# A long convolution and a spectral mixer on one core: two Z blocks share one buffer for their upper 52 rows, which are contracted in pairs of half height

## The chip, the cores and the metric

The kernel runs on one core of one Trainium2 chip. The metric is the device time of one execution in microseconds. A core has TensorE (PE; its weight loads are listed as PEld), VectorE (DVE), ScalarE (ACT), GpSimd (POOL), and SyncE (SP), which issues DMA transfers here. Sixteen DMA engines serve the core.

## The reference

The input x has 8 batches of 5696 positions and 128 channels. The first part is a causal convolution along the sequence with a filter h as long as the sequence, written as a product of spectra. The second part mixes the 64 lowest modes of the result's spectrum with complex 128 x 128 matrices, adds the mixed signal y to the convolution's result to get u, and returns u plus the positive part of u times a matrix.

```python
def _attn_ref(x, h):
    L = 2 * S
    Yf = np.fft.rfft(x, n=L, axis=1) * np.fft.rfft(h, n=L, axis=0)[None]
    return np.fft.irfft(Yf, n=L, axis=1)[:, :S]

def _moe_ref(x, w_r, w_i, w_ch):
    X = np.fft.rfft(x, axis=1)
    Xr, Xi = X.real[:, :64], X.imag[:, :64]
    Yr = einsum('bmd,mde->bme', Xr, w_r) - einsum('bmd,mde->bme', Xi, w_i)
    Yi = einsum('bmd,mde->bme', Xr, w_i) + einsum('bmd,mde->bme', Xi, w_r)
    u = x + np.fft.irfft(Yr + 1j * Yi, n=S, axis=1)
    return u + np.maximum(u @ w_ch, 0.0)
```

## The kernel before

The sequence index is split as 64 times 89. The batches go in four groups of two. For each group the kernel transforms along the 89 positions (As), then along the 64 (Xs), multiplies by the filter's spectrum (U), transforms back along the 64 (Z), and writes Z to a scratch tensor `zscr` in DRAM as 2 x 90 = 180 rows (real and imaginary parts of 90 frequencies) of 64 positions x 256 columns (two batches of 128 channels). A write covers four frequencies, so 23 of them, one per "tick", fill a group. On the way the 64 low modes of each batch are collected (XT). All four groups pass through these ticks; this ends at about 249 us.

**The last stage.** The modes are mixed with the weights (`mix`, result C), and then the convolution's result is made by contracting the 180 rows of Z with a constant table S4, while C times a table IBs adds the mixed modes into the same PSUM banks. The 64 positions of a group go in four *blocks* of ZB = 16 positions, so there are 16 blocks in all. A block's 180 rows do not fit the 128 partitions: rows 0 to 127 stand in a buffer ZT*a and rows 128 to 179 (RB = 52 rows) in ZT*b, from partition PB = 32 on. The 32 partitions below are cleared once by POOL (`clear_zt`), and the contraction of this part runs over 84 partitions. There are NC = 5 buffers of each kind. `load_zt(i)` issues the two transfers of a block on SP.

A *tile* (`u_tile`, called with the block, the batch b and the half) makes 8 positions in two PSUM banks: `u_c` gives one matmul with C for each bank, and `u_z` for each of the 8 positions one S4a matmul over 128 rows and one S4b matmul over 84 rows, each with 89 columns. ScalarE or VectorE then moves the tile to a buffer UT in SBUF, in runs of 8 elements. Sixteen tiles make a group. When a group's tiles are done, its output is made by `o_tile`: four matmuls with WI (the channel matrix beside an identity), the positive part on ScalarE (R), the sum on VectorE (O or Os), and a transfer to the output. These output tiles are interleaved with the tiles of the next group, one or two after each tile, by the list `todo`. There are seven large output buffers O, each holding two output tiles and written by one transfer of 512 KB, and four small ones Os.

Tiles rotate through four slots of two PSUM banks, which output tiles share. Engines work in order. Each reads its own list, and waits are semaphores that a recorder derives from what an operation reads and writes. SP too is in order: a load behind an output transfer that waits for VectorE waits as well. A load waits until its buffer's last reader on TensorE is done.

**What runs ahead.** The tables and the first blocks are loaded during the ticks of the last group, by the dictionary `early`: at tick 8 the table S4b, at tick 10 block 0, at tick 12 S4a, at tick 14 the identity Id and IBs, at tick 16 block 1, then blocks 3 and 2; block 4 follows after the ticks. The load of Id waits for two of the Z writes to land, so SP stands still there for a while. Only half of S4 and IBs is loaded; the other half follows by symmetry and is made on the chip by `reflect`, on VectorE for S4a and IBs and on ScalarE for S4b. Three tiles of block 0 are contracted ahead of C, in between the matmuls of `mix` (`u_z` with `alone`).

The order of a tile before is, for each bank, C and then S4a and S4b in turn:

```python
for hb in parts:
    if not alone:
        u_c(i, b, half, t, hb, True)
    for pl in range(4):
        for ri in range(2):          # S4a, S4b
            ...
            mm(pv(t + hb, pl * NQ, [[1, NQ]]), z[ri][0:n, ...], s4_sb[ri][0:n, so:so + NQ], ...)
```

Of the kernel before, what the change touches and what calls it, by code (L numbers as in the profile page):

```python
# [4 lines left out]
P = 128  # L5
F16 = mybir.dt.float16
# [117 lines left out]
def bass_long_conv_fft__then__afno_spectral_mix_kernel(nc, x, h, moe_w_r, moe_w_i, moe_w_ch, out):  # L124
# [37 lines left out]
    s4t = np.zeros((P, 2 * SH))  # L162
    s4t[:, 0:SH] = rows[0:P, 0:SH]
    s4t[PB:PB + RB, SH:2 * SH] = rows[P:2 * NK, 0:SH]
    sg = np.ones((P, 3))
    sr = np.stack([(-1.0) ** kk, -(-1.0) ** kk], axis=1).reshape(2 * NK)
    sg[:, 0] = sr[0:P]
    sg[PB:PB + RB, 1] = sr[P:2 * NK]
    sg[M:P, 2] = -1.0
    tt = np.arange(S)  # L170
# [38 lines left out]
    def take(nbytes):  # L209
# [40 lines left out]
    wc_sb = at("Wc", 2 * P, F16, take(2 * P * 2))  # L250
    sg_sb = at("SG", 3, F32, take(12))
# [4 lines left out]
    ZB = 16  # L256
# [4 lines left out]
    zt_off = [(a_h, a_h2), (a_as1, a_as1 + 2 * ZP), (a_as1 + 4 * ZP, a_as1 + 6 * ZP), (a_h + 2 * ZP, a_h2 + 2 * ZP),  # L261
              (a_m2, a_g)]
    assert 2 * S + 8 * ZP <= AW * 2
    zt = [[at(f"ZT{i}{'ab'[p_]}", ZP, F16, zt_off[i][p_]) for p_ in range(2)] for i in range(NC)]
    ib_sb = at("IBs", S, F16, a_m)
    s4_sb = [at("S4a", S, F16, a_m + 2 * S), at("S4b", S, F16, a_as)]
    assert 4 * S + 2 * ZP + 4 * P + 2048 <= 2 * MW
# [27 lines left out]
    R = Recorder(nc)  # L295
    for name, n in (("c", 16), ("x", 26), ("z", 10), ("w", 16), ("t", 20), ("s", 8), ("o", 12), ("p", 16), ("q", 10)):
        R.ring(name, n)
# [229 lines left out]
    ZX = [("zs", i, b) for i in range(NZ, NZL) for b in range(2)]  # L527
    zt_old = [(H_ALL, H_ALL), (AST, AST), (AST, AST), (H_ALL, H_ALL), (M_ALL[3:6], G_ALL)]

    def load_zt(i):  # L530
        g_, c_ = divmod(i, J // ZB)
        for part, (p0, r0, n) in enumerate(((0, 0, P), (PB, P, RB))):
            old = list(once(("zt", i % NC, part), zt_old[i % NC][part]))
            dma("sync", bass.AP(zt[i % NC][part], p0 * ZP, [[ZP, n], [1, ZP]]),
                bass.AP(zs, (g_ * 2 * NK + r0) * J * 256 + c_ * ZB * 256, [[J * 256, n], [1, ZP]]),
                "t", [("zd", g_, s_) for s_ in range(NT)], [("zt", i % NC, part)], after=old)

    def clear_zt(i):
        z32 = zt[i][1][0:PB, :].bitcast(U32)
        R.add("gpsimd", lambda e: e.memset(z32, 0), (), [("zt0", i)], after=list(zt_old[i][1]) + pace)  # L540

    def load_ib():
# [11 lines left out]
    def load_s4(part):  # L554
        n = PB + RB if part else P
        dma("sync", s4_sb[part][0:n, 0:SH], bass.AP(c_s4, part * SH, [[2 * SH, n], [1, SH]]), "p", (),
            [("s4", part, 0)], after=AST if part else M_ALL[1:4])
# [13 lines left out]
    pace = []  # L571

# [91 lines left out]
    def tick(g_, t):  # L664
# [27 lines left out]
        if LC <= t < NT + LC:  # L692
            s_ = t - LC
            n = len(ticks[s_])
            i, zi = s_ % NU, zroom(g_, s_)
            zb = [turns("z", ZBANK) for b in range(2)]
            for b in range(2):
                for r in range(2):
                    mm(pv(zb[b], 0, [[1, n * D]]), (W1, W2)[r], u_s[i][:, r * 1024 + b * 512:r * 1024 + b * 512 + n * D],
                       r == 0, r == 1, [("u", i), ("wc",)], [bank(zb[b])])  # L700
                evac(bass.AP(z_s[zi], b * D, [[1024, P], [2 * D, n], [1, D]]),
                     pv(zb[b], 0, [[D, n], [1, D]]), [bank(zb[b])], [("zs", zi, b)], eng="scalar",
                     after=once(("zx", zi, b), Z_OLD) if zi >= NZ else ())
                if b == 0:
                    drained(g_, t, 0)
            zo = (g_ * NK + KT * s_) * P * 256
            dma("sync", bass.AP(zs, zo, [[256, P], [P * 256, n], [1, 256]]),
                bass.AP(z_s[zi], 0, [[1024, P], [256, n], [1, 256]]), "z",
                [("zs", zi, 0), ("zs", zi, 1)], [("zd", g_, s_)])
# [39 lines left out]
    for g_ in range(NP):  # L749
# [3 lines left out]
        for t in range(NT + LM):  # L753
            tick(g_, t)
            assert g_ + 1 < NP or not wp
            if g_ == NP - 1 and t in early:
                pace[:] = [("u", min(t, NT - 1) % NU)]
                early[t]()
# [13 lines left out]

    pace[:] = []
    load_wi()
    for i in range(4, NC):
        load_zt(i)
        clear_zt(i)

# [4 lines left out]

    def u_z(i, b, half, alone=False, parts=(0, 1)):
        g_, c_ = divmod(i, NCH)
        t = ahead.get((i, b, half))
        if t is None:
            t = turns("l", LSLOT)
        z = zt[i % NC]
        for hb in parts:  # L790
            if not alone:
                u_c(i, b, half, t, hb, True)
            for pl in range(4):
                for ri in range(2):
                    pz = half * 8 + hb * 4 + pl
                    so = (c_ * ZB + pz) * NQ
                    n = (P, PB + RB)[ri]
                    mm(pv(t + hb, pl * NQ, [[1, NQ]]), z[ri][0:n, pz * 256 + b * P:pz * 256 + b * P + P], s4_sb[ri][0:n, so:so + NQ],
                       alone and pl == 0 and ri == 0, not alone and pl == 3 and ri == 1, [("zt", i % NC, ri), ("zt0", i % NC), ("s4", ri, 0)] + ([("s4", ri, 1)] if c_ >= NCH // 2 else []), [bank(t + hb)])
        if alone:  # L800
            ahead[(i, b, half)] = t
        return t

    def u_c(i, b, half, t, hb, first_):
        g_, c_ = divmod(i, NCH)
        pl0 = half * 8 + hb * 4
        mm(pv(t + hb, 0, [[1, 4 * NQ]]), c_sb[:, (2 * g_ + b) * P:(2 * g_ + b + 1) * P],
           ib_sb[:, (c_ * ZB + pl0) * NQ:(c_ * ZB + pl0 + 4) * NQ], first_, not first_,
           [("c", g_ // 2), ("ib", 0)] + ([("ib", 1)] if c_ >= NCH // 2 else []), [bank(t + hb)])

    def u_tile(i, b, half):
        g_, c_ = divmod(i, NCH)
        t = ahead.get((i, b, half))
        if t is None:
            t = u_z(i, b, half)
        else:
            for hb in range(2):
                u_c(i, b, half, t, hb, False)
        ub = (g_ % 2) * 2 + b
# [3 lines left out]
        src = pv(t, 0, [[1, NQ], [512, 2], [NQ, 4]])  # L823
        evac(bass.AP(u_sb[ub], c_ * ZB + half * 8, [[S, P], [J, NQ], [4, 2], [1, 4]]),
             src, [bank(t), bank(t + 1)], [("u_", ub, 2 * c_ + half)], eng=e, after=once(("u", ub), old))
# [32 lines left out]
    reflect("vector", ib_sb, P, 2, ("ib",), M_ALL[0:2])  # L858

# [52 lines left out]
    todo = []  # L912
    NB = NCH * NP
    NW4 = NW // 4
    for g_ in range(NP):
        last = g_ == NP - 1
        order = [(c_, b) for b in range(2) for c_ in range(NCH)] if last else [(c_, b) for c_ in range(NCH) for b in range(2)]
        for n, (c_, b) in enumerate(order):
            i = NCH * g_ + c_
            for half in range(2):  # L920
                u_tile(i, b, half)
                for _ in range((2, 2 + half)[n >= NCH] if last else 1 + half):
                    if todo:
                        o_tile(*todo.pop(0))
            if b == 1 and i + NC < NB:
                load_zt(i + NC)
            if last and n == NCH - 1:
                todo += [(g_, 0, r4) for r4 in range(NW4)]
# [37 lines left out]
```

## Time and profile before

| | us |
|---|---|
| Time, median of 3 runs | 372.31 (371.18 to 373.6) |
| Span of the profiled execution, first to last instruction | 370.1 |
| TensorE busy | 354.7 (96%) |
| ScalarE busy | 316.2 (85%) |
| VectorE busy | 291.8 (79%) |
| POOL busy | 75.2 (20%) |
| Chain that ended last: TensorE's share | 78% |

The profile is one execution; the runs were timed without it. A matmul's length in it reaches from its start to its modelled end, and matmuls overlap in the pipe, so the price of one is the distance between starts. The granted TensorE clock was 0.999 on average. Numbers behind "x" are counts.

### The profile page before, as it was taken

How to read it: one execution, taken by the hardware profiler on the slowest of the kernel's cores; microseconds unless marked ns; L12 is line 12 of the kernel's file. 1: busy time of each engine (PE TensorE's matmuls, PEld its weight loads, DVE VectorE, ACT ScalarE, POOL GpSimd, SP SyncE). 2: the span in 40 equal slices, each digit the busy share in tenths (PEclk: the TensorE clock that was granted, in tenths of full speed). 3: DMA queues.
4: the chain of work that ended last, by engine and by line, in shares of the span. 5: the costliest groups of instructions: out<-in, count | busy, mean ns of one | idle time of the engine just before them, and what ended most of it. 6: DMA issues, size and time to landing. Idle time of an engine off the chain costs nothing.

```text
span 370.1 us, 12455 instructions
## 1 busy us (share of the span) xinstructions
PE 354.7 (96%) x5350; PEld 276.5 (75%) x5350; DVE 291.8 (79%) x332; ACT 316.2 (85%) x499; POOL 75.2 (20%) x117
## 2 busy tenths in 40 slices
PE   7999899999999999999999999999999999999994
PEld 7878766667866668866668766668899888888873
DVE  3549899988999999989999988775357777756666
ACT  8559999999999999999999999995467777688885
POOL 8804012100833311823213001151000000000000
PEclk9999999999999999999999999999999999999999
DMA  7999979969999996999996999999999999999878
GB/s 139 209 271 382 249 165 292 232 198 283 93 140 213 263 258 186 132 160 215 263 278 128 171 310 363 342 345 388 381 410 386 413 410 408 418 399 376 326 291 349
DMA packets 87048, 103.94 MB, mean 281 GB/s; under 512 B 22730, under 2 KB 72522, under 8 KB 83438
## 3 DMA queue, kind: packets, MB, share of 16 engines
q1 hardware_dynamic: 64610, 81.33, 62.5%
q0 software_dynamic: 22384, 21.83, 35.4%
q8 instruction: 42, 0.69, 0.7%
q14 instruction: 12, 0.10, 0.1%
HBM read 70.61 MB, written 51.12 MB: 329 GB/s over the span
## 4 chain that ended last, share of the span: by engine, by line
PE 78%; ACT 10%; DMA 7%; DVE 3%; issue 1%; POOL 1%; DVEq 0%; POOLq 0%
PE ps L323 78%; ACT As L313 6%; DMA out_dram<-O 5%; DMA Hin<-in_h_dram 2%; ACT R L898 1%; DVE As L317 1%; ACT Xs L311 1%; DVE U L623 1%; POOL Hin L320 1%; ACT UT L311 1%; DVE O L899 0%; ACT Zs L311 0%; DVE Hp L438 0%; ACT C L313 0%; DVE Hs L315 0%
## 5 line engine op out<-in xcount | busy, mean ns | idle before, releaser
L652 DVE TENSOR_TENSOR U<-Xs,Hs 128x2048 f16<-128x2048 f16 (+1 forms) x72 | 85.8, 1197 | 12.1 <-ACT Xs L311 11.5
L323 PE MATMUL ps<-U,Wc 128*128 128x512 f16 (+1 forms) x368 | 93.8, 376 | 1.4 <-DVE U L623 1.4
L311 ACT CAST Xs<-ps 128x1024 f16<-128x1024 f32 (+1 forms) x76 | 75.0, 995 | 5.8 <-PE ps L323 3.1
L311 ACT CAST Zs<-ps 128x512 f16<-128x512 f32 (+1 forms) x132 | 70.1, 605 | 0.7
L899 DVE TENSOR_TENSOR O<-ps,R 128x512 f32<-128x512 f32 x81 | 52.4, 684 | 21.6 <-ACT R L898 11.4
L898 ACT ACTIVATE R<-ps 128x512 f32<-128x512 f32 (+1 forms) x92 | 50.5, 592 | 8.5 <-PE ps L323 8.4
L317 DVE TENSOR_SCALAR As<-ps 128x720 f16<-128x720 f32 x64 | 53.1, 879 | 4.8 <-PE ps L323 3.3
L323 PE MATMUL ps<-As,M 64*128 64x128 f16 (+3 forms) x1504 | 52.5, 214 | 2.4 <-ACT As L313 1.2
L313 ACT ACTIVATE As<-ps 128x720 f16<-128x720 f32 (+1 forms) x68 | 48.2, 771 | 5.0 <-PE ps L323 4.8
L323 PE MATMUL ps<-F,Xin 128*128 128x180 f16 x512 | 52.1, 249 | 0.1
L323 PE MATMUL ps<-WI,UT 128*128 128x256 f16 x360 | 50.8, 278 | 0.5 <-ACT UT L311 0.4
L311 ACT CAST UT<-ps 128x712 f16<-128x712 f32 x46 | 34.5, 752 | 19.4 <-PE ps L323 18.4
L323 PEld LDWEIGHTS ps<-U,Wc 128*128 128x128 f16 x368 | 29.1, 97 | 28.2 <-DVE U L623 1.9
L323 PEld LDWEIGHTS ps<-F,Xin 128*128 128x128 f16 x512 | 45.2, 155 | 6.7 <-DVE Xin L365 0.9
L323 PEld LDWEIGHTS ps<-As,M 64*128 64x128 f16 x1504 | 42.2, 94 | 8.7 <-ACT Xs L311 1.9
L323 PEld LDWEIGHTS ps<-WI,UT 128*128 128x128 f16 x360 | 38.9, 152 | 3.2 <-issue 1.8
L323 PE MATMUL ps<-IBs,C 128*128 128x356 f16 x128 | 39.2, 314 | 0.8 <-DVE O L899 0.7
L320 POOL DMA_DIRECT2D Xt<-in_x_dram x40 | 21.4, 540 | 76.5 <-PE ps L323 76.0
L323 PEld LDWEIGHTS ps<-G,Zs 128*128 128x128 f16 x512 | 26.1, 96 | 14.1 <-ACT Zs L311 0.2
L652 DVE TENSOR_TENSOR U<-ps,Hs 128x2048 f16<-128x2048 f32 (+1 forms) x16 | 35.5, 2216 | 0.0
L323 PE MATMUL ps<-G,Zs 128*128 128x128 f16 (+2 forms) x512 | 31.9, 192 | 0.1
L311 ACT CAST Zt<-ps 128x512 f16<-128x512 f32 x52 | 29.1, 659 | 0.0
(76 smaller groups left out, 479.4 us busy)
## 6 DMA issues: line engine op xcount, KB each, us to landing
out_dram<-O SPq DMA_DIRECT2D x39, 512.0 KB, 10.5
zscr<-Zs SPq DMA_DIRECT2D x62, 256.0 KB, 6.7
zscr<-Zt SPq DMA_DIRECT2D x26, 256.0 KB, 6.6
Xt<-in_x_dram POOLq DMA_DIRECT2D x20, 320.0 KB, 6.9
W<-wscr SPq DMA_DIRECT2D x4, 1024.0 KB, 8.5
ZT0a<-zscr SPq DMA_DIRECT2D x4, 1024.0 KB, 11.0
M<-cM POOLq DMA_DIRECT2D x5, 720.0 KB, 17.6
ZT1a<-zscr SPq DMA_DIRECT2D x3, 1024.0 KB, 11.1
```

Of the source, the lines that this page charges most:

```text
L311: R.add(e, lambda h_: h_.copy(dst, src), reads, writes, after=after)
L313: R.add(e, lambda h_: h_.activation(dst, src, COPY, scale=scale), reads, writes, after=after)
L317: R.add(e, lambda h_: h_.tensor_scalar_mul(dst, src, scale), reads, writes, after=after)
L320: R.add(eng, lambda h_: h_.dma_start(dst, src), reads, writes, ring=ring, after=after)
L323: R.add("tensor", lambda h_: h_.matmul(o, l, r, start=st, stop=sp), reads, writes)
L623: R.add("vector", lambda e: e.tensor_tensor(bass.AP(u_s[0], b * 512 + d0, [[2048, P], [1024, 2], [D, n], [1, d1 - d0]]), bass.AP(s_[0], s_ ...
L652: R.add("vector", lambda e: e.tensor_tensor(uv, src, hv, MULT), bk + [("h", t, 0), ("h", t, 1, 0), ("h", t, 1, J)], [("u", i)])
L898: R.add("scalar", lambda e: e.activation(rv, src_r, RELU), bk, [("r", i % NR)], after=once(("r", i % NR), G_ALL + XTT + [("y", 0), ("y", 1 ...
L899: R.add("vector", lambda e: e.tensor_tensor(ov, src_u, rv, ADD), bk + [("r", i % NR)], [key + (h_,)], after=once(key, old))
```

## The change

- The upper 52 rows of two neighbouring blocks share one buffer ZB*: block 2k from partition 0, block 2k+1 from partition PB = 64. There are NCB = 3 such pair buffers, and NCA = 7 buffers ZA* for the lower 128 rows of single blocks.
- A tile now covers 4 positions of each of the two blocks of a pair instead of 8 positions of one, so a pair has 8 tiles. Its order is: C for both banks, four S4a matmuls for the one block, four for the other, and then for each position the two S4b matmuls, one on partitions 0-51 and one on 64-115, one behind the other. Each of these has 52 rows and is built for a half-height (64-row) position of the array.
- The table S4b is laid out to match, over S/2 columns and both partition halves, and is loaded whole. Its reflection on ScalarE is gone, and so are the clears on POOL.
- The last write of each group (tick 22, two frequencies, 4 rows) goes to a scratch tensor of its own, `zlast`, whose pieces of 256 elements stand 264 apart. A pair buffer is therefore loaded, for each of its two blocks, by one transfer of 48 rows and four transfers of one row in sixteen pieces of 512 bytes: ten transfers for a pair. They use a ring "r" of 16 semaphores of their own.
- The loads move: at tick 10 ZA for block 0 and the first pair buffer, at tick 16 ZA for block 1, at tick 19 ZA for block 2 and the second pair buffer, at tick 21 ZA for block 3, after the ticks ZA for block 4, the third pair buffer, and ZA for blocks 5 and 6. Later, at the end of each pair, the next pair buffer and two ZA.
- UT is written in runs of 4 elements, 16 apart, instead of runs of 8.

```diff
-    RB, PB = 2 * NK - P, 32
+    RB, PB = 2 * NK - P, 64
+    RS = RB % 16
...
+    for p0 in range(2):
+        s4b[p0 * PB:p0 * PB + RB] = rows[P:].reshape(RB, J // ZB // 2, 2, ZB * NQ)[:, :, p0].reshape(RB, S // 2)
...
+    ZLW = 2 * D + 8
+    zl = nc.dram_tensor("zlast", [NP * RS * J, ZLW], F16, kind="Internal")
...
-    NC = 5
+    NCA, NCB = 7, 3
...
-    def load_zt(i):
...
-    def clear_zt(i):
...
+    def load_za(i):
+        g_, c_ = divmod(i, J // ZB)
+        r_ = i % NCA
+        dma("sync", za[r_][:, :], bass.AP(zs, g_ * 2 * NK * J * 256 + c_ * ZP, [[J * 256, P], [1, ZP]]),
+            "t", zdone(g_), [("za", r_)], after=once(("za", r_), za_old[r_]))
+
+    def load_zb(k):
+        r_ = k % NCB
+        for p0 in range(2):
+            g_, c_ = divmod(2 * k + p0, J // ZB)
+            n = RB - RS
+            dma("sync", bass.AP(zb_[r_], p0 * PB * ZP, [[ZP, n], [1, ZP]]),
+                bass.AP(zs, (g_ * 2 * NK + P) * J * 256 + c_ * ZP, [[J * 256, n], [1, ZP]]),
+                "t", zdone(g_), [("zb", r_, p0)], after=once(("zb", r_, p0), zb_old[r_]))
+            for r in range(n, RB):
+                dma("sync", bass.AP(zb_[r_], (p0 * PB + r) * ZP, [[ZP, 1], [256, ZB], [1, 256]]),
+                    bass.AP(zl, ((g_ * RS + r - n) * J + c_ * ZB) * ZLW, [[J * ZLW, 1], [ZLW, ZB], [1, 256]]),
+                    "r", zdone(g_), [("zr", r_, p0, r)], after=once(("zr", r_, p0, r), zb_old[r_]))
...
-             9: lambda: clear_zt(0),
-             10: lambda: load_zt(0),
+             10: lambda: (load_za(0), load_zb(0)),
              12: lambda: load_s4(0),
-             14: lambda: (load_id(), load_ib(), clear_zt(1)),
-             16: lambda: load_zt(1),
-             19: lambda: (load_zt(3), clear_zt(3)),
-             NT - 2: lambda: (load_zt(2), clear_zt(2))}
+             14: lambda: (load_id(), load_ib()),
+             16: lambda: load_za(1),
+             19: lambda: (load_za(2), load_zb(1)),
+             NT - 2: lambda: load_za(3)}
...
+        for hb in range(2 if 0 in parts else 0):
+            z, r_ = za[(2 * k + hb) % NCA], (2 * k + hb) % NCA
             for pl in range(4):
...
+                mm(pv(t + hb, pl * NQ, [[1, NQ]]), z[:, pz * 256 + b * P:pz * 256 + b * P + P], s4_sb[0][:, so:so + NQ],
+                   alone and pl == 0, False, [("za", r_)] + ns, [bank(t + hb)])
+        r_ = k % NCB
+        for pl in range(4 if 1 in parts else 0):
...
+            for hb in range(2):
+                r0 = hb * PB
+                mm(pv(t + hb, pl * NQ, [[1, NQ]]), zb_[r_][r0:r0 + RB, pz * 256 + b * P:pz * 256 + b * P + P],
+                   s4_sb[1][r0:r0 + RB, so:so + NQ], False, not alone and pl == 3,
+                   [("zb", r_, hb), ("s4", 1, 0)] + [("zr", r_, hb, r) for r in range(RB - RS, RB)], [bank(t + hb)])
...
-    reflect("scalar", s4_sb[1], PB + RB, 1, ("s4", 1), AST)
...
             if b == 1:
+                if k + NCB < NPR * NP:
+                    load_zb(k + NCB)
+                for i in (2 * k, 2 * k + 1):
+                    if i + NCA < NCH * NP:
+                        load_za(i + NCA)
```

More of the change, by code (lines that the diff above doesn't have):

```diff
@@ L527, in bass_long_conv_fft__then__afno_spectral_mix_kernel, with zdone @@
     ZX = [("zs", i, b) for i in range(NZ, NZL) for b in range(2)]
-    zt_old = [(H_ALL, H_ALL), (AST, AST), (AST, AST), (H_ALL, H_ALL), (M_ALL[3:6], G_ALL)]
-    def load_zt(i):
-        g_, c_ = divmod(i, J // ZB)
[L532 to L536, printed above, removed]
-    def clear_zt(i):
-        z32 = zt[i][1][0:PB, :].bitcast(U32)
-        R.add("gpsimd", lambda e: e.memset(z32, 0), (), [("zt0", i)], after=list(zt_old[i][1]) + pace)
+    za_old = [H_ALL, AST, H_ALL, AST, AST, M_ALL[3:6], G_ALL]
+    zb_old = [H_ALL, H_ALL, AST]
+    def zdone(g_):
+        return [("zd", g_, s_) for s_ in range(NT)]
+    def load_za(i):
+        g_, c_ = divmod(i, J // ZB)
+        r_ = i % NCA
[13 more added lines that the diff above has]
+                    "r", zdone(g_), [("zr", r_, p0, r)], after=once(("zr", r_, p0, r), zb_old[r_]))
     def load_ib():
@@ L554, in load_s4 @@
     def load_s4(part):
-        n = PB + RB if part else P
-        dma("sync", s4_sb[part][0:n, 0:SH], bass.AP(c_s4, part * SH, [[2 * SH, n], [1, SH]]), "p", (),
+        w = S // 2 if part else SH
+        dma("sync", s4_sb[part][:, 0:w], bass.AP(c_s4, part * SH, [[SH + S // 2, P], [1, w]]), "p", (),
             [("s4", part, 0)], after=AST if part else M_ALL[1:4])
@@ L770, in bass_long_conv_fft__then__afno_spectral_mix_kernel @@
                     dma("gpsimd", dst, src_, ring, (), [tok], after=[("as", j)])
-    pace[:] = []
     load_wi()
-    for i in range(4, NC):
-        load_zt(i)
-        clear_zt(i)
+    load_za(4)
+    load_zb(2)
+    load_za(5)
+    load_za(6)
     LSLOT = [0, 2, 4, 6]
@@ L782, in bass_long_conv_fft__then__afno_spectral_mix_kernel, with u_z @@
     ahead = {}
-    def u_z(i, b, half, alone=False, parts=(0, 1)):
-        g_, c_ = divmod(i, NCH)
-        t = ahead.get((i, b, half))
+    def u_z(k, b, h4, alone=False, parts=(0, 1)):
+        g_, c_ = divmod(2 * k, NCH)
+        t = ahead.get((k, b, h4))
         if t is None:
             t = turns("l", LSLOT)
[L789 to L792, printed above, removed]
-            for pl in range(4):
[L794 to L799, printed above, removed]
+        if not alone:
+            for hb in range(2):
+                u_c(k, b, h4, t, hb, True)
+        ns = [("s4", 0, 0)] + [("s4", 0, 1)] * (c_ >= NCH // 2)
+        for hb in range(2 if 0 in parts else 0):
+            z, r_ = za[(2 * k + hb) % NCA], (2 * k + hb) % NCA
+            for pl in range(4):
+                pz = h4 * 4 + pl
+                so = ((c_ + hb) * ZB + pz) * NQ
+                mm(pv(t + hb, pl * NQ, [[1, NQ]]), z[:, pz * 256 + b * P:pz * 256 + b * P + P], s4_sb[0][:, so:so + NQ],
+                   alone and pl == 0, False, [("za", r_)] + ns, [bank(t + hb)])
+        r_ = k % NCB
+        for pl in range(4 if 1 in parts else 0):
+            pz = h4 * 4 + pl
+            so = (c_ // 2 * ZB + pz) * NQ
+            for hb in range(2):
+                r0 = hb * PB
+                mm(pv(t + hb, pl * NQ, [[1, NQ]]), zb_[r_][r0:r0 + RB, pz * 256 + b * P:pz * 256 + b * P + P],
+                   s4_sb[1][r0:r0 + RB, so:so + NQ], False, not alone and pl == 3,
+                   [("zb", r_, hb), ("s4", 1, 0)] + [("zr", r_, hb, r) for r in range(RB - RS, RB)], [bank(t + hb)])
@@ L800, in u_z, with u_c @@
         if alone:
-            ahead[(i, b, half)] = t
+            ahead[(k, b, h4)] = t
         return t
-    def u_c(i, b, half, t, hb, first_):
-        g_, c_ = divmod(i, NCH)
-        pl0 = half * 8 + hb * 4
+    def u_c(k, b, h4, t, hb, first_):
+        g_, c_ = divmod(2 * k, NCH)
         mm(pv(t + hb, 0, [[1, 4 * NQ]]), c_sb[:, (2 * g_ + b) * P:(2 * g_ + b + 1) * P],
-           ib_sb[:, (c_ * ZB + pl0) * NQ:(c_ * ZB + pl0 + 4) * NQ], first_, not first_,
+           ib_sb[:, ((c_ + hb) * ZB + h4 * 4) * NQ:((c_ + hb) * ZB + h4 * 4 + 4) * NQ], first_, not first_,
@@ L912, in bass_long_conv_fft__then__afno_spectral_mix_kernel @@
     todo = []
-    NB = NCH * NP
+    NPR = NCH // 2
     NW4 = NW // 4
@@ L916, in bass_long_conv_fft__then__afno_spectral_mix_kernel @@
         last = g_ == NP - 1
-        order = [(c_, b) for b in range(2) for c_ in range(NCH)] if last else [(c_, b) for c_ in range(NCH) for b in range(2)]
+        order = [(c_, b) for b in range(2) for c_ in range(NPR)] if last else [(c_, b) for c_ in range(NPR) for b in range(2)]
         for n, (c_, b) in enumerate(order):
[L919 to L922, printed above, removed]
+            k = NPR * g_ + c_
+            for h4 in range(4):
+                u_tile(k, b, h4)
+                for _ in range((2, 2 + h4 % 2)[n >= NPR] if last else 1 + h4 % 2):
                     if todo:
                         o_tile(*todo.pop(0))
-            if b == 1 and i + NC < NB:
-                load_zt(i + NC)
-            if last and n == NCH - 1:
+            if b == 1:
+                if k + NCB < NPR * NP:
[3 more added lines that the diff above has]
+                        load_za(i + NCA)
+            if last and n == NPR - 1:
                 todo += [(g_, 0, r4) for r4 in range(NW4)]
```

46 lines of the change are left out of this document (22 added, 24 removed).

## The prediction

> **What bounds the kernel now.** I read the chain of waits first, then the busy times by stretch, then the list of waits from 230 us on, then single tiles of the last stage in the timeline. The change touches only that last stage (from about 249 us) and the loads that feed it (from 224 us).
>
> The chain, in order of time: start, length, what.
>
> ```profile
> span 370.1 us, 12455 instructions
> ...
> 249.94 4.86 PE ps L323 x152
> ...
> 262.63 54.98 PE ps L323 x816
> ...
> 320.68 16.68 DMA out_dram<-O
> ...
> 338.32 7.48 PE ps L323 x100
> ```
>
> From 262.63 to 317.61 the chain is TensorE alone, with no gap. Then it runs through an output transfer of 16.68 us, which a buffer waits for, and from 338.32 through TensorE again. The stretches (PE, PEld, DVE, ACT, POOL busy, granted clock, DMA share, GB/s):
>
> ```profile
> 220.00:240.00 20.00, 20.00 (x314) 13.03 (x314) 16.45 (x13) 19.57 (x32) 3.59 (x2) 1.00 1.05 353
> 300.00:320.00 20.00, 19.73 (x285) 17.70 (x284) 14.07 (x22) 14.74 (x26) 0.00 (x0) 1.00 1.02 410
> 320.00:340.00 20.00, 19.41 (x258) 16.85 (x257) 12.96 (x20) 16.06 (x28) 0.00 (x0) 1.00 0.97 395
> ```
>
> TensorE is busy in 19.73 of 20 us and at the same time the DMA engines are full (share 1.02). So there are two limits side by side: TensorE sets the pace, the transfers are only just not late. What was late at all from 230 us on is in the waits (total us, times, longest):
>
> ```profile
> PEld ps L323 <- issue: 3.5, 17, 0.4
> PEld ps L323 <- DMA ZT0b<-zscr: 0.4, 1, 0.4
> PE ps L323 <- DVE O L899: 0.7, 2, 0.4
> SPq L320 <- DVE O L899: 55.2, 41, 3.8
> SPq L320 <- DMA zscr<-Zt: 3.7, 1, 3.7
> ```
>
> TensorE lost 0.4 us to a load and 0.7 us to a full output buffer; the SP queue, which issues all these transfers in order, mostly waits for VectorE's results.
>
> **The tile of the last stage, now and after.** One tile pair without its output part, and the output matmuls behind it, up to the next tile:
>
> ```profile
> 290.54 0.31 PE L323 MATMUL ps<-IBs,C 128*128 128x356 f16 x1
> 290.69 0.20 PE L323 MATMUL ps<-S4a,ZT2a 128*128 128x89 f16 x1
> ...
> 290.98 0.20 PE L323 MATMUL ps<-S4b,ZT2b 84*128 84x89 f16 x1
> 291.03 0.31 PE L323 MATMUL ps<-IBs,C 128*128 128x356 f16 x1
> 291.18 0.20 PE L323 MATMUL ps<-S4a,ZT2a 128*128 128x89 f16 x1
> ...
> 291.48 0.20 PE L323 MATMUL ps<-S4b,ZT2b 84*128 84x89 f16 x1
> 291.52 0.62 PE L323 MATMUL ps<-WI,UT 128*128 128x256 f16 x4
> ...
> 291.98 0.31 PE L323 MATMUL ps<-IBs,C 128*128 128x356 f16 x1
> ```
>
> The 0.20 us are the length of one matmul in the pipe; its price is the distance of starts. Eight matmuls (4 S4a, 4 S4b) start between 290.69 and 291.03: 0.042 us each. The tile costs 2 x 0.15 + 16 x 0.042 = 0.98 us. There are 64 tiles (4 groups of 16), so the 512 S4b matmuls cost 512 x 0.042 = 21.5 us, all on the chain.
>
> After the change a tile has the same two C matmuls and eight S4a matmuls, and the eight S4b matmuls become four pairs, one on rows 0-51 and one on rows 64-115, into different banks. The kernel already does this: the As matmuls with 64 rows go in such pairs. What a pair costs, and what it costs to go from full height to half height and back, stands in the ticks before:
>
> ```profile
> 59.96 0.41 PE L323 MATMUL ps<-Ah,M 64*128 64x64 f16 x16
> 60.20 0.61 PE L323 MATMUL ps<-As,M 64*128 64x128 f16 x16
> ...
> 221.89 0.50 PE L323 MATMUL ps<-G,Zs 128*128 128x2 f16 x8
> 222.32 1.07 PE L323 MATMUL ps<-As,M 64*128 64x128 f16 x32
> 223.32 0.39 PE L323 MATMUL ps<-U,Wc 128*128 128x512 f16 x1
> ...
> 231.16 0.49 PE L323 MATMUL ps<-G,Zs 128*128 128x2 f16 x8
> 231.49 0.81 PE L323 MATMUL ps<-U,Wc 128*128 128x512 f16 x3
> ...
> L323 PE MATMUL ps<-As,M 64*128 64x128 f16 x1376 | 48.8, 217 | 0.5 <-ACT Xs L311 0.5
> L323 PE MATMUL ps<-G,Zs 128*128 128x128 f16 x256 | 28.4, 217 | 0.0
> ```
>
> *The pair.* Eight pairs of 64 columns take 59.96 to 60.20, 0.030 us a pair. Sixteen pairs of 128 columns: (1.07 - 0.217) / 15 = 0.057 us a pair. For 89 columns, in proportion between the two, 0.040 us. Four pairs are 0.16 us in place of 8 x 0.042 = 0.34 us: 0.18 us a tile, 11.3 us in all, if nothing else were paid.
>
> *The switch.* The last of the G matmuls (0.217 long, full height) starts at 221.89 + 0.50 - 0.217 = 222.17, and the first As matmul (half height) at 222.32: 0.15 us later. Without a change of height, the same G matmul at 231.16 + 0.49 - 0.217 = 231.43 is followed by the next at 231.49: 0.06 us. On the way back the last As starts at 222.32 + 1.07 - 0.217 = 223.17, the first U matmul at 223.32: 0.15 us against 0.057 us for a pair. Each switch costs 0.09 us. Before, the last stage had none; after, each tile has two (S4a to the pairs, pairs to the next C or WI matmul): 0.18 us a tile.
>
> So the tile pays 0.16 + 0.18 = 0.34 us for what cost 0.34 us. Unrounded it is 4 x 0.0405 + 0.09 + 0.093 against 8 x 0.0425, +0.005 us a tile, **+0.3 us** in all; an error of 0.01 us in each of a switch, a pair and a single matmul makes it -1.3 to +1.9.
>
> [...]
>
> **The loads that come first.** Before, the first tiles needed block 0 alone. Now one tile covers blocks 0 and 1, so the first one, at 248.85, also needs block 1's upper rows.
>
> ```profile
> 238.59 0.33 SPq L320 DMA_DIRECT2D Id<-cW  x1
> ...
> 241.31 0.56 SPq L320 DMA_DIRECT2D ZT1a<-zscr  x1
> ...
> 248.85 0.20 PE L323 MATMUL ps<-S4a,ZT0a 128*128 128x89 f16 x1
> ...
> DMA to landing us min/median/max: 7.7/11.1/12.4
> ...
> S4b<-cS SPq DMA_DIRECT2D x1, 481.9 KB
> ZT0b<-zscr SPq DMA_DIRECT2D x4, 416.0 KB
> ```
>
> The landing line is that of ZT1a, the first being the shortest: 241.31 + 7.7 = 249.0. In the queue ahead of it the change puts the second half of the first pair buffer (416 KB) and a larger S4b (128 x 2848 x 2 bytes = 712 KB for 482 KB): 646 KB or 0.66 MB more, with the engines full. At 353 GB/s that is 1.9 us, at 410 GB/s 1.6 us: block 1 lands at 250.6 to 250.9. Then four S4a matmuls, a switch, four pairs and a switch (0.17 + 0.09 + 0.16 + 0.09 = 0.51 us) stand before the mode mixing, which started at 249.94 and now starts at 251.1 to 251.4. The mixing leads to C, and all evictions of the stage wait for C. I take **+1.4 us**; 0 if the queue catches up in SP's pause before 238.59, 2.2 at most if SP is late too.
>
> **Smaller parts.** *Waits:* a pair's first use waits for 12 completions in place of 4, eight times. Nearest row: 3.5 us in 17 for TensorE's own issue, 0.2 us each; eight make 1.6 us, part falls into the switch: **+0.6** (0 to 1.6). *Eviction:* UT is now written in runs of 4 elements, not 8.
>
> ```profile
> L311 ACT CAST UT<-ps 128x712 f16<-128x712 f32 x46 | 34.5, 752 | 19.4 <-PE ps L323 18.4
> L313 ACT ACTIVATE As<-ps 128x720 f16<-128x720 f32 x64 | 46.6, 787 | 5.0 <-PE ps L323 4.8
> ```
>
> As is written in runs of 4: 1.093 ns an element against 1.056 for UT. That would be 26 ns on 46 evictions, 1.2 us, where ScalarE is not the limit nothing: **+0.2** (0 to 1.2). *Third pair:* blocks 4 and 5 are wanted together, block 5 four tiles sooner; the longest wait for a load was 0.4: **+0.3** (0 to 0.6). *Relief:* loads go out earlier, so the 0.4 us for ZT0b and part of the 0.7 us for O can go, the latter also because TensorE comes later: **-0.6** (0 to -0.7). *Costed at nothing:* the five clears on POOL (nothing waits for POOL), the reflection of S4b on ScalarE (the chain is TensorE's in that time; without that cover it would be a gain), and 64 more issues on SP, because SP waits 55.2 us for VectorE; what they cost if that cover is thin is the second rival.
>
> **Sum.** 1.4 + 0.3 + 0.6 + 0.2 + 0.3 - 0.6 = +2.2 us: span 372.3. The median of the runs, 372.31, lies 2.2 us over the span of the profile, so I forecast **374.5 us**, 0.6% slower. All lower ends together give -2.0 (370.3), all upper ends +7.5 (379.8). The measurement tells about 1% (3.7 us) from no change, so this counts as the same.
>
> **Rivals.**
>
> *The switches hide (faster).* If the array were refilled behind the eight S4a matmuls, 11.3 us would go from TensorE, 358.8 us of span. But the transfers are full (1.02, 410 GB/s), and the output buffer that came free at 337.36 would bind: only the tiles after it, about ten of the last group's sixteen, give 0.18 us each, 1.8 us, and the waits of 0.7 and 0.4 us; late loads would no longer matter. Between 358.8 and 367.2 I take 366.5, nearer the transfers' end: **368.7 us**. Against it: both switches cost 0.09 us in the ticks. [...]
>
> *SP's burst (slower).* At one place, the tick that loads the first pair, SP issues ten transfers where it issued one, ahead of the remaining Z writes, Id, IBs and block 1. What an issue takes on that queue (ns, min/median/max):
>
> ```profile
> L320 SPq DMA_DIRECT2D ZT0b<-zscr x4: 449/672/1400, 228.9 to 319.6; - x4
> ```
>
> Nine more issues have a cover of 3.7 us, SP's wait before 238.59, and 1.6 us by which block 1 is late anyway: from 5.3 / 9 = 0.59 us an issue on, SP decides. At the minimum of 0.45 us they are hidden. At 1.0 us, between median and maximum, block 1 comes 3.7 us later still: 376.0 us of span, **378.2 us**; at 1.4 us it is 7.3 us, 381.8 us.
>
> *The pairs run one after the other (the change doesn't do what it says).* Then the switches are paid for nothing: 64 x 0.18 = 11.5 us, **386 us**. Against it: the As pairs at 0.057 us for 128 columns each.
>
> **Chances.** Forecast 0.58 (of which 0.08 beyond 1%), switches hidden 0.12, SP's burst 0.27, pairs in series 0.03. So faster 0.12, same 0.50, slower 0.38. The range runs from 369.5, which leaves out most of the first rival, to 381.0; about 0.18 lies outside.
>
> **What would show it.** In the timeline of a tile: pairs of S4b starts a few ns apart, pairs 0.040 us apart, 0.14 us from the last S4a to the first S4b, 0.98 us for a tile. Block 1 landing at 250.6 and the mixing starting at 251.1 to 251.4. The first load wait of TensorE on a ZA tile, about 1.5 us, at 249. The chain still TensorE from 263 to 318. Wrong: a tile of 0.82 us (switches hidden), an SP queue still issuing the first pair after 235 us, or pairs 0.08 us apart.

## The result and the profile after

The changed kernel takes 396.09 us (median; 394.26 to 397.12) against 372.26 us for the kernel before in the same session. The ratio is 1.0635, with a 95% interval of 1.0591 to 1.068: 6% slower, far outside the range of 369.5 to 381.0. Where some executions of a run below were in a slower state of the chip, its median and its ratio leave them out.

The chain of waits of the changed kernel, in order of time (start, length, what):

```profile
span 392.5 us, 12539 instructions
...
245.36 8.96 DMA ZA<-zscr
...
255.02 6.46 PE ps L327 x159
...
264.81 7.51 PE ps L327 x128
273.68 0.59 SPq L324
...
287.76 19.87 DMA out_dram<-O
...
326.73 13.39 DMA out_dram<-O
...
350.06 19.64 PE ps L327 x258
```

Where the chain of before was TensorE alone for 55 us, it now leaves TensorE three times for long: to SP's queue, in many short pieces from 273.68 to 287.72, and to two output transfers of 19.87 and 13.39 us. The stretches of the changed kernel (PE, PEld, DVE, ACT, POOL busy, granted clock, DMA share, GB/s):

```profile
264.00:300.00 36.00, 32.71 (x480) 25.67 (x478) 16.98 (x23) 19.32 (x31) 0.00 (x0) 0.95 1.04 280
300.00:320.00 20.00, 13.84 (x177) 10.65 (x175) 9.46 (x14) 8.94 (x16) 0.00 (x0) 0.83 1.02 359
320.00:340.00 20.00, 18.35 (x248) 15.44 (x248) 11.42 (x17) 13.44 (x23) 0.00 (x0) 1.00 1.03 376
```

And the first of these stretches in the kernel before:

```profile
264.00:300.00 36.00, 36.00 (x545) 32.36 (x542) 23.24 (x34) 24.25 (x40) 0.00 (x0) 1.00 1.01 405
```

The first of the three rows and this one are to be read together. The DMA engines are full in both kernels (shares 1.04 and 1.01), but they move 280 GB/s where they moved 405. A share says how much of the time an engine holds a packet, not how fast the packet goes. In single packets of the trace, one of 8192 bytes took 309 ns in the kernel before (median, 270 to 300 us) and about 530 ns in the changed one. TensorE, which worked through this stretch before, now waits in it and in the next. Waits of the changed kernel from 230 us on (total us, times, longest; TensorE's in the rows that begin with PE), where the two rows on ZA are the same two waits, seen by the weight loads and by the matmuls:

```profile
PEld ps L327 <- issue: 10.4, 15, 5.6
DVE O L918 <- DMA out_dram<-O: 9.4, 2, 6.3
PE ps L327 <- DVE O L918: 7.5, 2, 5.4
...
PEld ps L327 <- DMA ZA<-zscr: 4.8, 2, 3.4
PE ps L327 <- DMA ZA<-zscr: 4.5, 2, 3.2
```

How the 22.4 us of span divide is read from the last product U of the ticks and the first and last UT. Before:

```profile
L652 DVE TENSOR_TENSOR U<-ps,Hs x16: 1218/2283/2284, 107.0 to 246.1; 128x2048 f16<-128x2048 f32 x15, 128x1024 f16<-128x1024 f32 x1
...
L311 ACT CAST UT<-ps x46: 752/752/758, 257.2 to 357.3; 128x712 f16<-128x712 f32 x46
```

After:

```profile
L664 DVE TENSOR_TENSOR U<-ps,Hs x16: 1217/2282/2284, 109.1 to 248.6; 128x2048 f16<-128x2048 f32 x15, 128x1024 f16<-128x1024 f32 x1
...
L315 ACT CAST UT<-ps x46: 752/755/765, 263.9 to 379.9; 128x712 f16<-128x712 f32 x46
```

The ticks end 2.5 us later (246.1, 248.6), the mixing takes 4.2 us longer (11.1 us from the last U to the first UT, now 15.3), the tile loop 15.9 us longer (100.1, now 116.0), and the end 0.2 us less (12.8, now 12.6). The first 2.5 us belong for the most part to the execution, as the next section shows. The loss is in the loop.

### The profile page after: what moved, and what is told of

Read it like the earlier page. It is cut to its first block, busy times and chain, and to the rows that moved or that the text cites. A ratio compares the mean times of both kernels' runs of the same rounds, so it can differ in the third digit from the quotient of the medians.

```text
span 392.5 us, 12539 instructions
## 1 busy us (share of the span) xinstructions
PE 360.7 (92%) x5350; PEld 272.5 (69%) x5350; DVE 291.0 (74%) x332; ACT 314.0 (80%) x498; POOL 67.0 (17%) x112
## 4 chain that ended last, share of the span: by engine, by line
PE 58%; DMA 17%; ACT 10%; DVE 6%; SPq 4%; issue 3%; POOL 1%; DVEq 0%; POOLq 0%
PE ps L327 58%; DMA out_dram<-O 8%; ACT As L317 6%; SPq L324 4%; DMA Hs<-Hs 3%; DMA ZA<-zscr 2%; DMA Hin<-in_h_dram 2%; DMA Xt<-in_x_dram 2%; ACT Xs L315 2%; DVE Hs L319 2%; DVE As L321 1%; DVE Xin L369 1%; DVE U L635 1%; POOL Hin L324 1%; ACT Zs L315 1%
## 5 line engine op out<-in xcount | busy, mean ns | idle before, releaser
L327 PE MATMUL ps<-WI,UT 128*128 128x256 f16 x360 | 53.3, 287 | 1.8 <-ACT UT L315 1.7
L327 PEld LDWEIGHTS ps<-S4a,ZA 128*128 128x128 f16 x512 | 29.7, 101 | 12.2 <-DMA ZA<-zscr 4.8
L327 PE MATMUL ps<-S4a,ZA 128*128 128x89 f16 x512 | 33.6, 209 | 4.7 <-DMA ZA<-zscr 4.5
L327 PE MATMUL ps<-IBs,C 128*128 128x356 f16 x128 | 30.4, 324 | 7.8 <-DVE O L918 7.5
```

The lines of the kernel that those rows point to most:

```text
L327: R.add("tensor", lambda h_: h_.matmul(o, l, r, start=st, stop=sp), reads, writes)
```

## The experiments

Each run was timed against the kernel before on the same chip. The first four take the change's transfers apart.

**One transfer a half (one52).**

```diff
-            dma("sync", bass.AP(zs, ...) if s_ < NT - 1 else bass.AP(zl, ...), ...)
+            dma("sync", bass.AP(zs, ...), ...)
...
-            n = RB - RS
+            n = RB
...
-            for r in range(n, RB):
-                dma("sync", bass.AP(zb_[r_], (p0 * PB + r) * ZP, [[ZP, 1], [256, ZB], [1, 256]]), bass.AP(zl, ...), "r", ...)
```

> The changed kernel, but the last tick is written into zscr as before and each half of a pair buffer is filled by one 52-row transfer: no zlast and none of its 64 one-row transfers, everything else kept. Theory I (issue: SP's ten issues a pair buffer, 0.59 us a one-row transfer, hold up the loads and outputs behind them): 372 to 378 us. Theory R (rows: the one-row sixteen-piece transfers themselves slow the DMA engines, 8192-B packets at 530 ns in place of 309): also 372 to 378, and the packets back at 309. Theory S (shape: the 48-row transfers, three rows on each of the 16 engines): also near 374, as this shape goes too. Theory A (the pairs, the order of loads, the prefetch depth: nothing to do with the split): stays at 390 to 396.

Measured: 389.02 us, ratio 1.0458 (1.0396 to 1.0521). Against its own kernel before it is 17.3 us slower, the change 23.8: only 6.5 us go with the 64 one-row transfers and the 48-row shape, and theories I, R and S, which all gave about 372 to 378, are refuted as the main cause. The rate stays low:

```profile
264.00:300.00 36.00, 31.40 (x452) 24.88 (x447) 15.78 (x23) 18.97 (x30) 0.00 (x0) 0.91 1.01 321
```

Theory A gave 390 to 396 and comes nearest. But this row speaks against the pairs as the cause: the DMA engines are full (1.01) and move 321 GB/s, which work on TensorE does not explain.

**The 48 rows alone (only48).**

```diff
-            for r in range(n, RB):
-                dma("sync", bass.AP(zb_[r_], (p0 * PB + r) * ZP, ...), ...)
...
-                mm(..., zb_[r_][r0:r0 + RB, ...], s4_sb[1][r0:r0 + RB, ...], ...)
+                mm(..., zb_[r_][r0:r0 + RB - RS, ...], s4_sb[1][r0:r0 + RB - RS, ...], ...)
```

> The changed kernel without the 64 one-row transfers, the 48-row transfers kept; the contraction of each pair uses 48 rows, so rows 176 to 179 are left out of the result. Theories I and R: 372 to 378 us, 8192-B packets at about 309 ns. Theory S (the shape of the 48-row transfers): 390 or more, packets still near 500 ns in the stretches in which the ZB tiles load. Theory A: 390 to 396.

Measured: 390.61 us, ratio 1.0492 (1.0452 to 1.0531), rate 287 GB/s in the same stretch. Both sizes of the large transfer, 48 and 52 rows, are slow without any one-row transfer.

**The one-row transfers from POOL (rows_pool).**

```diff
-                dma("sync", bass.AP(zb_[r_], (p0 * PB + r) * ZP, ...), ...)
+                dma("gpsimd", bass.AP(zb_[r_], (p0 * PB + r) * ZP, ...), ...)
```

> The changed kernel with the 64 one-row transfers issued on POOL instead of SP: the same packets in the same places, SP has two issues a pair buffer in place of ten. Theory I: 373 to 380 us, with the first output issued near 275 us again. Theory R: 390 to 398, the 8192-B packets slow as before even though SP is free. Theories S and A: 390 to 398 too.

Measured: 397.63 us, ratio 1.0693 (1.0653 to 1.0733), no better than the change. SP's queue, freed of 64 issues, reaches the first output little sooner (the first row is this run, the second the kernel before):

```profile
286.22 9.24 SPq L324 DMA_DIRECT2D out_dram<-O  x5
...
275.01 4.37 SPq L320 DMA_DIRECT2D out_dram<-O  x3
```

In the changed kernel that row starts at 287.76. So theory I falls: what holds up the outputs is not SP's time for issues.

**The split put into the kernel before (before_split).**

```diff
-        for part, (p0, r0, n) in enumerate(((0, 0, P), (PB, P, RB))):
+        for part, (p0, r0, n) in enumerate(((0, 0, P), (PB, P, RB - RS))):
...
+        for r in range(RB - RS, RB):
+            dma("sync", bass.AP(zt[i % NC][1], (PB + r) * ZP, [[ZP, 1], [256, ZB], [1, 256]]), bass.AP(zl, ...), "r", ...)
```

> The kernel before with nothing changed but the transfer of rows 128 to 179: 48 rows from zscr and four one-row transfers in sixteen pieces from zlast for each of the 16 blocks; one block's buffer each at partitions 32 to 83, contraction over 84 rows, no pairs. Theory I: 380 to 392 us (five issues a block in place of one; the bursts are half as long and come twice as often). Theory R: 388 to 398. Theory S: 388 to 398. Theory A: 371 to 375.

Measured: 389.87 us, ratio 1.0497 (1.0438 to 1.0557), with no pair in it. That refutes theory A, which gave 371 to 375, and the rate shows the same loss:

```profile
264.00:300.00 36.00, 32.70 (x473) 28.68 (x470) 18.30 (x26) 20.24 (x33) 0.00 (x0) 0.95 1.03 295
```

So there were two facts to join. Two transfers of 52 rows are slow in the changed kernel (321 GB/s in the run with one transfer a half), and one transfer of 52 rows is fast in the kernel before (405). They differ in the partitions that they write: 0 to 51 and 64 to 115, against 32 to 83. That is theory P: where the rows lie decides, because the engines of one transfer hinder each other at some places and not at others. The reason given was the author's assumption; no trace shows it.

**The same kernel, other partitions (before_at64).**

```diff
-    RB, PB = 2 * NK - P, 32
+    RB, PB = 2 * NK - P, 64
...
-        n = PB + RB if part else P
+        n = P
```

> The kernel before with one number changed: rows 128 to 179 lie at partitions 64 to 115 in place of 32 to 83 (partitions 0 to 63 zero). Same transfers of 52 rows by 13 engines, same bytes, no pairs, no zlast, one issue a block. [...] Theory N (the number or order of transfers and SP's issues): packets at 309, 370 to 374 us.

Measured: 394.92 us, ratio 1.0583 (1.0516 to 1.0649), against the 370 to 374 of theory N. The new place in the kernel before costs 22.0 us, nearly as much as the whole change. The second edit loads the table S4b over 128 partitions instead of 84, once; that is 0.26 MB more, 0.6 us at 410 GB/s by an estimate, and not the cause:

```profile
264.00:300.00 36.00, 30.45 (x438) 26.99 (x439) 17.13 (x25) 18.45 (x30) 0.00 (x0) 0.93 1.02 305
```

**The pairs with loads of 128 rows (pairs_wide and pairs_bytes).**

```diff
-        for p0 in range(2):
-            dma("sync", bass.AP(zb_[r_], p0 * PB * ZP, [[ZP, 52], [1, ZP]]), ...)
+        dma("sync", zb_[r_][:, :], bass.AP(zs, g_ * 2 * NK * J * 256 + c_ * ZP, [[J * 256, P], [1, ZP]]), ...)
```

In the second run a row of the transfer is 13 * 256 elements long, and the pairs read the positions modulo 13.

> The run with one 52-row transfer a half, its two transfers replaced by one of 128 rows to 128 partitions, which is the shape and place of the ZA loads; the pairs, the order of loads and the array's work stay. The rows are rows 0 to 127 of one block, so what the pairs contract is not the reference's, and 24 more rows a buffer are moved (8 x 24 x 8 KB). Theory P: packets at 309 ns again and 373 to 380 us. Theory A (the pairs or the order of loads cost it): 386 to 391 us as with the 52-row halves.

> The run with one 128-row transfer a pair buffer, with rows of 6.5 KB in place of 8 KB (13 of 16 blocks, so that its bytes are those of two halves of 52 rows); the pairs read what is there, so what they contract is not the reference's. It leaves of the change the pairs, the modes and the order of loads, with the transfers' rate intact. If the array's part and the order cost what the prediction's sum says: 374.5, 373 to 376 us. If the 24 extra rows were nothing and the array's part cost the 3.9 us: 376 to 378. If the pairs gain: below 371.

Measured: 376.79 us, ratio 1.0118 (1.0065 to 1.0171), and with the bytes of the change 374.39 us, ratio 1.0047 (1.0015 to 1.0078). The rate of the first is back, and so is its chain of TensorE alone:

```profile
264.00:300.00 36.00, 36.00 (x546) 29.27 (x543) 21.74 (x31) 22.85 (x37) 0.00 (x0) 1.00 1.02 423
```

```profile
243.53 8.98 DMA ZA<-zscr
252.56 6.79 PE ps L327 x164
...
262.70 88.46 PE ps L327 x1262
```

That refutes theory A. The change without its small transfers (their place, their number and `zlast`) costs 2.5 us by the medians, and 0.6 to 2.9 us by the interval.

**A deal to twelve engines (split_12x4), a run that did not do what it was meant to.**

```diff
+            rows_ = [[4 * J * 256, 12], [J * 256, 4]] if part else [[J * 256, n]]
...
-                bass.AP(zs, ..., [[J * 256, n], [1, ZP]]), ...
+                bass.AP(zs, ..., rows_ + [[1, ZP]]), ...
```

> The kernel before with 48 rows and four one-row transfers from zlast, as in the run of that split, but the 48 rows dealt to 12 engines by four in place of 16 engines by three, still at partitions 32 to 79; only the source's pattern is written differently. Theory P: the 48-row packets come back to 309 ns, and the time from 389.9 to 374 to 382, the rest being the price of the one-row transfers. Theory R (one-row transfers slow the engines): stays at 386 to 392.

Measured: 391.29 us, ratio 1.0477 (1.0421 to 1.0534). The semaphore of the first such transfer rises sixteen times with the data, between 237.64 and 240.53 us, as in the plain split, so the rows still went to 16 engines by three. The run says nothing on the deal.

**A second profile of the kernel before (before_again).**

> The kernel before, unchanged, for a second profile: whether the 1.6 to 2.4 us by which the changed kernel's profile is late from 66 to 79 us on, long before the change, belong to the execution (theory: this profile shows them too, or a part) or to the change (this profile is at 76.5 us at the same instruction, as the first).

```profile
L652 DVE TENSOR_TENSOR U<-ps,Hs x16: 1218/2284/2285, 108.1 to 248.0; 128x2048 f16<-128x2048 f32 x15, 128x1024 f16<-128x1024 f32 x1
...
L311 ACT CAST UT<-ps x46: 752/752/758, 259.1 to 357.8; 128x712 f16<-128x712 f32 x46
```

It is at 78.1 us at the instruction in question, a product U on VectorE. Its ticks end at 248.0, 1.9 us after those of the first profile, and its span is 370.3 us all the same: the loop made it up. So being late by 2 us before the change's place is in the execution, and it costs nothing by itself.

**Two more places (before_at44 and before_at48).** Each is the edit of the run at 64 with another number: 44 (partitions 44 to 95) and 48 (48 to 99).

> The kernel before with rows 128 to 179 at partitions 44 to 95 in place of 32 to 83, nothing else. [...] If only the old place 32 is good, or any change of place or of the addresses costs something: 380 to 395.

> [...]

Measured: 390.94 us, ratio 1.0534 (1.0482 to 1.0585), and 393.18 us, ratio 1.0583 (1.0535 to 1.0632). Theory P falls here. It had assumed that at 44 to 95 the engines of a transfer would not hinder each other, and the time was nearly as bad as at 64 (the rate was 293 GB/s against 305; at 48 it was 279):

```profile
264.00:300.00 36.00, 29.52 (x450) 26.00 (x448) 15.64 (x22) 19.94 (x32) 0.00 (x0) 1.00 1.02 293
```

**The one-row transfers alone (plus_rows).**

```diff
+        for r in range(RS):
+            dma("sync", bass.AP(zt[i % NC][1], (PB + RB + r) * ZP, [[ZP, 1], [256, ZB], [1, 256]]), bass.AP(zl, ...), "r", ...)
```

> The kernel before in full, and on top of it four one-row sixteen-piece transfers a block (64 in all) from a padded scratch, into partitions 84 to 87 of the b buffers, which nothing reads, and one more store of the last tick a group. The 52-row transfers stay at 32 to 83. It prices the one-row transfers alone. Theory R (they slow the DMA queue) and theory I (SP's issue time): 380 to 392 us. If they cost their own packets (64 x 16 of 512 B at 27 to 48 ns and 64 x 16 semaphore writes at 9 to 16 ns, 2.3 to 4 us of the 16 engines): 374 to 378.

Measured: 378.54 us, ratio 1.0192 (1.0142 to 1.0242). That is 6.7 us for 64 transfers (and four stores), 0.10 us each: just above the 374 to 378 us of their own packets, and below the 380 to 392 us of theories R and I. It is near the 6.5 us between the change and the run with one transfer a half.

**Who writes what (theory O).** In the kernel before, the semaphore of the first 52-row transfer rises once at its issue (229.55 us) and 13 times with the data (234.94 to 237.82), which is read here as 13 engines with four rows each; transfers of 44, 8, 48 and 64 rows in the runs below and above give 11, 8, 16 and 16. Which rows an engine takes no trace shows. Theory O assumes that the first engine takes the first rows, the next the next ones, and that a transfer is slow when its engines write other partitions than they do in the fast transfer of 52 rows from partition 32 on. From 44 on each engine is then three groups of four off. Three runs test that. In the first, 44 of the rows go ahead of the other 8, so that the engines of the 44 stay where they were. In the second the 8 go first, and the engines of the 44 are two groups off. In the third the rows are at 44, but one transfer of 64 rows from partition 32 on puts each engine back.

```diff
 deal_44_8:
-        for part, (p0, r0, n) in enumerate(((0, 0, P), (PB, P, RB))):
+        for tok, p0, r0, n in ((0, 0, 0, P), (1, PB, P, 44), (2, PB + 44, P + 44, 8)):
 deal_8_44:
+        for tok, p0, r0, n in ((0, 0, 0, P), (1, PB, P, 8), (2, PB + 8, P + 8, 44)):
 at44_own (on the run at 44):
-        for part, (p0, r0, n) in enumerate(((0, 0, P), (PB, P, RB))):
+        for part, (p0, r0, n) in enumerate(((0, 0, P), (32, P - 12, RB + 12))):
```

> [...] It is the control for the next. Theory O and theory L both: 8192-B packets at 309 ns in the main, 372 to 378 us (one issue more a block).

> [...] Place, rows, bytes and issues are those of the control. Theory O (which engine writes which partitions): packets near 500 ns or more, 384 to 394 us. Theory L (the place 32 to 83 is good): 372 to 378 us as the control.

> [...] 12 rows more a block (16 x 12 x 8 KB = 1.57 MB, 3.8 us at 410 GB/s). Theory O: packets back at 309 ns, 374 to 379 us. Theory L: packets near 500 ns, 391 to 398 us.

Measured: 378.95 us (1.0152, 1.0083 to 1.0222), 391.0 us (1.0484, 1.0384 to 1.0585) and 372.71 us (1.0008, 0.9969 to 1.0047). The control is 1 us above its range of 372 to 378, the third run below its 374 to 379. The first two write the same rows to the same partitions with the same number of issues, and differ by 12 us through the order of the two sizes. The third leaves the rows where they cost 390.94 us, moves 1.57 MB more, and is as fast as the kernel before. Its rate and its chain, in a profile of its slowest execution (376.29 us):

```profile
264.00:300.00 36.00, 33.30 (x484) 29.63 (x483) 19.42 (x28) 20.89 (x35) 0.00 (x0) 0.95 1.01 395
```

```profile
266.08 30.41 PE ps L323 x444
...
297.18 34.88 PE ps L323 x497
```

Theory L, the place, is refuted by both comparisons. Each alone leaves a rival (a small transfer ahead of a large one; 13 engines in place of 16), but the first does not touch the runs at 44, and the kernel before is fast on 13 engines. The runs whose loads of Z are of 52 or 64 rows from partition 32 on, or of 128 rows, and to which no one-row transfer is added, took 371.7 to 376.8 us, at 395 to 423 GB/s in that stretch. Those with 52 rows from another partition on, with 48 rows, or with 8 rows ahead of 44 took 389.0 to 397.6 us, at about 280 to 320 GB/s. The control took 379 us at 380 GB/s; its eight rows go by a transfer of their own, and it has one issue more a block, and which of the two cost its 6.4 us was not tried. Theory O agrees with the first two of these groups but says nothing on loads of 128 rows. Which engine wrote which partition is not in the trace, so its deal stays an assumption of the author's.

## Why the prediction was wrong

**The tile was right.** The tile behind 301.12 us, the counterpart of the one shown before:

```profile
301.12 0.47 PE L327 MATMUL ps<-IBs,C 128*128 128x356 f16 x2
301.42 0.50 PE L327 MATMUL ps<-S4a,ZA 128*128 128x89 f16 x8
301.85 0.34 PE L327 MATMUL ps<-S4b,ZB 52*128 52x89 f16 x8
302.13 1.10 PE L327 MATMUL ps<-WI,UT 128*128 128x256 f16 x8
```

It takes 302.13 - 301.12 = 1.01 us; 0.98 was forecast. The last S4a starts at 301.42 + 0.50 - 0.20 = 301.72, the first pair 0.13 us later (forecast 0.14), and three distances of pairs are 0.34 - 0.20 = 0.14 us, 0.047 each (0.040). So the switches eat what the pairs save. Over 64 tiles the 0.03 us above the forecast would be 1.9 us, an estimate that the tile loop without the small transfers, shown next, does not bear out: it is no longer than before. The first rival (switches hidden) and the third (pairs in series) are out.

**The late block 1 was mis-sized.** The forecast was +1.4 us, with 2.2 at most. In the changed kernel the mixing stretch grew by 4.2 us. Without any of the small transfers, in the run with 128-row loads, it is 14.8 us:

```profile
L658 DVE TENSOR_TENSOR U<-ps,Hs x16: 1218/2284/2286, 107.8 to 246.9; 128x2048 f16<-128x2048 f32 x15, 128x1024 f16<-128x1024 f32 x1
...
L315 ACT CAST UT<-ps x46: 752/756/767, 261.8 to 361.3; 128x712 f16<-128x712 f32 x46
L319 DVE CAST UT<-ps x18: 880/892/900, 261.7 to 326.0; 128x712 f16<-128x712 f32 x18
```

That is 261.7 - 246.9, 3.7 us more than the 11.1 of before. The wait for block 1 itself is 2.3 us where about 1.5 was forecast (the waits of that run from 245 to 262 us; what TensorE waits for is ZA, block 1's lower 128 rows, whose landing the forecast used though it spoke of the upper ones):

```profile
PEld ps L327 <- DMA ZA<-zscr: 2.3, 1, 2.3
```

What the step left out is the clock. The stretches of the same run:

```profile
252.00:254.00 2.00, 1.44 (x24) 1.18 (x25) 0.00 (x0) 0.00 (x0) 0.00 (x0) 0.60 1.14 414
254.00:256.00 2.00, 2.00 (x41) 2.00 (x39) 0.00 (x0) 0.00 (x0) 0.00 (x0) 0.55 1.02 428
```

And the run with one transfer a half, which had block 1 at 251.8 and waited 0.6 us for it, with the piece of its chain that begins there:

```profile
252.00:254.00 2.00, 2.00 (x65) 1.85 (x63) 0.90 (x2) 0.00 (x0) 0.00 (x0) 1.00 1.14 397
...
251.82 5.44 PE ps L327 x164
```

After the wait TensorE was granted 0.60 and 0.55 for 4 us, and its piece of the chain, shown above, took 6.79 us. The same 164 matmuls took 5.44 us at the full clock, so 1.35 us are the clock's. The other 0.6 us over the 4.86 of before are 12 matmuls more. The piece also starts 1.8 us later behind the last U (252.56 - 246.9, before 249.94 - 246.1), and with these three the 3.7 us are complete. The gap between the two matmuls at that wait was 2.1 us. In the run with one transfer a half the whole stretch from the last U to the first UT is 11.2 us. The loop then gave a little back: 361.3 - 261.7 = 99.6 us against 100.1. So the 374.39 us of the run with the change's bytes lies at the forecast of 374.5, but not by the forecast's terms: in the run traced here the late block cost 3.7 us where 1.4 were forecast, and the loop gained 0.5 us where the other terms together gave +0.8. That the errors nearly cancel is luck.

**The step that failed** is "costed at nothing", with what stood behind it: of the small transfers only the issues on SP were weighed there, and the rate was taken to stay at 353 to 410 GB/s, wherever a load lands. The sum has no term for a lower rate, though the prediction had found the transfers "only just not late", so that a lower rate had to reach TensorE. The rate fell from 405 to 280 GB/s, and the tile loop grew by 15.9 us. The trace of before could not show it, since all its loads of Z are of 128 rows, or of 52 from partition 32 on. That 48 rows go to 16 engines and 52 to 13, by the rises of their semaphores, did not help: the run with the 48 rows alone moved 287 GB/s.

**SP's burst, the slower rival, had the right sign and the wrong mechanism.** Its threshold was 0.59 us an issue, and the issues took just that (min/median/max ns):

```profile
L324 SPq DMA_DIRECT2D ZB<-zlast x64: 481/588/1592, 231.1 to 339.7; - x64
L324 SPq DMA_DIRECT2D ZB<-zscr x16: 427/578/1122, 230.6 to 337.2; - x16
```

SP did issue the first pair until 237.1, past the 235 us that were named as a sign, and block 1 landed at 245.36 + 8.96 = 254.3, not 250.6. But with those issues on POOL the time stayed at 397.63 us, and the stretch from the last U to the first UT went only from 15.3 to 14.1 us. The rival's price, 378 to 382 us, is near what the one-row transfers cost on their own (378.54), by coincidence: that run has no late block 1.

**The sum as measured.** By medians, each against its own kernel before: 2.5 us for the pairs, the order and the late block (374.39 less 371.88); 14.8 more for the two 52-row halves (389.02 less 371.69 is 17.3); 6.5 more for the 48-row shape with one-row transfers (396.09 less 372.26 is 23.8).

**Still open** is why the packets are slower where the rate is low (about 530 ns for 309 in the changed kernel); no run shows the cause. Nor was it told apart in the kernel before whether a one-row transfer's 0.10 us is SP's time or that of the 16 engines on one partition (its semaphore rises 16 times).

## What to carry to other kernels

Read the DMA share and the GB/s together: here a full share at a lower rate was slower packets (530 ns for 309), and neither bytes nor issues explained it. When a transfer's rows move to other partitions or its row count changes, measure its packets anew, or keep to a kind that the fast transfers of the profile already have (here 52 or 64 rows from partition 32 on, at 405 and 395 GB/s, or all 128, at 423). Before working on half-height pairs, price two switches of height against the matmuls saved: with four pairs between two switches nothing was left.

## What the hardware showed that was not expected

Where a 52-row transfer begins is worth a quarter of the DMA rate: 405 GB/s from partition 32 on against 293 and 305 from 44 and 64 on, with S4b loaded over more partitions, once. Twelve more rows a block were free (372.71 us with 1.57 MB more); the semaphore of their transfer rises 16 times where that of 52 rows rises 13 times, so three engines more may have taken them, which was not tested. After a wait of 2.3 us the granted clock was 0.60 and 0.55 for 4 us, and the same 164 matmuls took 1.35 us longer than at the full clock (6.79 for 5.44), more than half the wait once more.
